# Top-k attention with two MLP blocks: staging of the early scores, the values' middle chunk, and the place of the end flag

## The chip, the cores and the metric

The kernel runs on one core of one Trainium2 chip. The metric is the device time of one execution in microseconds (us), the median of several runs. The engines are called as in the profile: PE (TensorE, matmul), DVE (VectorE), ACT (ScalarE), POOL (GpSimd), SP (SyncE, which issues all the DMAs of this kernel).

## What is computed

Four batches, eight heads, 576 positions, head size 64, all in fp32. Each score row keeps its 32 largest entries. The attention's output goes through a gated block (a causal convolution of five taps makes the gate) and then through a token and a channel MLP.

```python
scores = scale * np.matmul(q, k.transpose(0, 1, 3, 2))
kth = np.partition(scores, -top_k, axis=-1)[..., -top_k:-top_k + 1]
scores = np.where(scores >= kth, scores, -1e9)
attn = softmax(scores)
x = np.matmul(attn, v)                      # (B, S, 512) after the heads are joined
gate = 1 / (1 + np.exp(-causal_conv5(x, conv_w)))
x = (gate * (x @ w_val)) @ w_out
u = x + (np.maximum(x.transpose(0, 2, 1) @ w_tok1, 0) @ w_tok2).transpose(0, 2, 1)
out = u + np.maximum(u @ w_ch1, 0) @ w_ch2
```

## The kernel before

The program is written by a planner. Every operation is added to an `Order` with its engine, an assumed cost, the keys that it reads and writes, and a priority. `Order.issue` (L143) makes eight rounds of list scheduling, forwards and backwards, keeps the shortest plan, and emits the instructions in the plan's order. On the chip each engine then runs its own instructions strictly in that order: an instruction that has to wait holds back all that stand behind it on its engine.

Work is cut by batch b, by pair p of heads (four pairs to a batch) and by unit u (five to a pair). A unit u < 4 is two tiles of 128 query rows, one per head; the unit u = 4 is one tile that holds the last 64 rows of both heads. `all` (L782) adds, for each batch, the 20 units of attention (`attn`, L372), then the gated block (`gate`, L606), then the token and channel MLP (`mix`, L691). The attention of batch b + 1 is planned beside gate and mix of batch b. Nothing stands beside the attention of batch 0 but the decoding of weights; nothing but gate and mix is left at the end.

One unit goes like this. `scores` (L301) makes q·k in two halves of 288 columns: PE writes PSUM (`Sp`, or in batch 0 `Sp` and `mo[0]` in turn), ACT copies each half to SBUF (`S`, L332, or L349 for u = 4), and the second half's product must wait for the first half's copy, since it takes the same PSUM. Between the halves DVE folds the row (`fold`, L468) and then finds the 32 largest (`topk`, L481 to L500). ACT makes the mask (L414), POOL applies it (L416), ACT takes the exponential and its sum (L419), PE transposes it (L428), ACT copies that (L433), PE multiplies by the values (`pv`, L439 to L445), and ACT moves the result to `xf` (L449).

Three places matter here.

- **Early scores.** Batch 3's scores are made already in batch 0's attention, one unit of `pre` (L358) after each unit of `attn`, with `pq` (queries and keys), `mo[1]` (PSUM) and a single tile `pst` into which ACT copies both halves. One DMA (L370) writes `pst` to a DRAM tile `sd`, which batch 3 reads back in place of its own score products (L389). The next unit's first copy may write `pst` only when that DMA has landed. `gate` of batch 0 takes `mo[0]` and `mo[1]` after them. The tiles `fs` (`f0` to `f3`), the running x of gate and mix, hold nothing until the gate of batch 0.
- **The values.** `vt` holds ten chunks of 64 columns: chunk 0 to 4 for one head, 5 to 9 for the other (shifted by 64 rows). For u < 4 `pv` issues eight products of 128 rows by 64 columns (L441, L442; one fp32 product shows as two records) and two on 64 by 64 (L444, L445) for the middle chunk, where the two heads share a chunk of rows.
- **The flag.** `fold` and `topk` leave in `bad` whether any row of any unit broke the shortcut. After the whole plan, `run` (L765) reduces `bad` on DVE (L771), transposes on PE (L772), reduces again (L773), compares (L775). All five engines load the flag (`values_load`, L776) and branch over a second, slow version of the program (L777).

Of the kernel before, what the change touches and what calls it, by code (L numbers as in the profile page):

```python
# [10 lines left out]
I32 = mybir.dt.int32  # L11
# [156 lines left out]
class Builder:  # L168
    def __init__(self, ctx, tc, qk, v, w_val, conv, w_out, w_tok1, w_tok2, w_ch1, w_ch2, out):
# [10 lines left out]
        self.vt = [T(f"v{i}", [128, 10, 64]) for i in range(2)]  # L180
# [13 lines left out]
        self.cst = T("cst", [1, 1])  # L194
# [15 lines left out]
        self.pq, self.pst = T("pq", [128, 2, S]), T("pst", [128, 2, S])  # L210
# [11 lines left out]
        self.cnt = dict(mo=0, tf=0, ring=0, rT=0, st=0, wa=0, unit=0, tile=0, load=0)  # L222
# [82 lines left out]
    def scores(self, u, Sp, kSp, q, k, P, R, St, kS, then):  # L305

        nc = self.nc
        if u < 4:

            for n in range(2):  # L310
# [19 lines left out]
                if n:  # L330
                    then()
                self.act(S, lambda c0=c0: nc.scalar.activation(St[:, :, c0:c0 + 288], Sp[:, :, 0:288], AF.Copy),  # L332
# [15 lines left out]
        for n in range(2):  # L348
            self.act(288, lambda n=n: nc.scalar.activation(St[:, 0, 288 * n:288 * n + 288], Sp[:, n, 0:288], AF.Copy),  # L349
                     [kSp], kS[n] + [kSp] * n)  # L350
            if n == 0:
                then()
# [5 lines left out]
    def pre(self, c, u):  # L358

        nc = self.nc  # L360
        t = self.pq
        R = [("pq", x) for x in range(2)]
# [4 lines left out]
        st = self.pst  # L367
        k = [("pst", x) for x in range(2)]
        self.scores(u, self.mo[1], ("mo", 1), t[:, 0], t[:, 1], None, R, st, [k[n:n + 1] for n in range(2)], lambda: None)
        self.dma(2.3 * w, lambda: nc.sync.dma_start(self.sd[c, u], st[:, 0:w]), k, [("sd", c, u)])  # L370

    def attn(self, p, u):  # L372
# [13 lines left out]
        if b == PRE and self.fast:  # L386
            x = (p % 4, u)
            o = St[:, 0:w]
            self.dma(2.3 * w, lambda x=x, o=o: nc.sync.dma_start(o, self.sd[x]), [("sd", *x)],  # L389
# [49 lines left out]
        def pv():  # L439
            for y in range(4):  # L440
                nc.tensor.matmul(o[0:64, 0:n], vt[:, y], a[:, y * 128:y * 128 + n], start=(y == 0), stop=False)  # L441
                nc.tensor.matmul(o[64:128, 0:n], vt[:, 5 + y], e[:, y * 128 + g:y * 128 + 128], start=(y == 0), stop=False)  # L442
            r = slice(64, 128) if w == 2 else slice(0, 64)
            nc.tensor.matmul(o[0:64, 0:n], vt[0:64, 4], e[0:64, 512:512 + n], start=False, stop=True)  # L444
            nc.tensor.matmul(o[64:128, 0:n], vt[r, 4 if w == 2 else 9], e[r, 512 + g:640], start=False, stop=True)  # L445

        self.pe(1.39 if w == 2 else 0.877, pv, [x[1] for x in pts] + [("v", s)],
# [317 lines left out]
    def run(self):  # L765
        nc = self.nc
        with self.tc.manual_schedule():
            self.setup()
            self.all(True)
            m = self.nb[0][:, 0, 0:1]  # L770
            nc.vector.tensor_reduce(m, self.bad, mybir.AxisListType.XYZ, OP.max)  # L771
            nc.tensor.transpose(self.PT[0:1, 0:128], m, self.ident)  # L772
# [4 lines left out]
        with self.tc.If(again == 1):  # L777
            with self.tc.manual_schedule():
                self.o = Order()
                self.all(False)  # L780
# [70 lines left out]
```

## Time and profile before

| | us |
|---|---|
| median of 3 runs | 940.01 |
| the 3 runs | 930.69, 940.01, 940.73 |
| the profiled execution, its own time | 931.29 |
| its span, first to last instruction | 929.4 |
| PE busy | 844.8 (91%) |
| DVE busy | 767.3 (83%) |
| ACT busy | 574.1 (62%) |
| POOL busy | 410.8 (44%) |
| mean granted clock of PE, of full speed | 0.964 |

Busy time counts the instructions of an engine and not its waits. A stretch in which an engine is busy nearly all the time is bound by it; where no engine is, the order in which the engines wait for one another sets the pace. Line numbers are those of the kernel before.

### The profile page before, as it was taken

To read this page: it belongs to the slowest core of one execution; us is meant where nothing else is said; L and a number is where in the kernel's file an instruction comes from. 1 tells how busy PE (TensorE), PEld (TensorE's weight loads), DVE (VectorE), ACT (ScalarE), POOL (GpSimd) and SP (SyncE) were. 2 spreads that over 40 slices of the span, in tenths; PEclk is the share of its full clock that TensorE was granted. 3 is DMA by queue.
4 is the path that set the end of the run, shared out by engine and by line. 5 is a ranking of instruction groups with operands and counts; after the bars stand their busy time and mean duration, and the time that the engine had idled before them with its cause. 6 is when DMAs were issued, how large, how long until landed. Compare 5 with 4: busy or idle time off the path is not lost.

```text
span 929.4 us, 18849 instructions
## 1 busy us (share of the span) xinstructions
PE 844.8 (91%) x6713; PEld 718.7 (77%) x6713; DVE 767.3 (83%) x2653; ACT 574.1 (62%) x1271; POOL 410.8 (44%) x369
## 2 busy tenths in 40 slices
PE   5777777998999998989999999989999999889996
PEld 2444445797887987769788888979799998879996
DVE  8789979788999999997699998999899997712222
ACT  4878796856887775685677675474665665322100
POOL 1333354776976676474264332274353443402000
PEclk8999895999999998989999999999999999999998
DMA  5434321256335545614213324743345545222452
GB/s 190 168 119 153 127 70 52 96 204 226 117 106 196 187 184 189 228 53 130 78 31 124 106 84 148 239 145 129 105 156 200 189 132 165 91 91 91 160 162 98
DMA packets 39496, 128.22 MB, mean 138 GB/s; under 512 B 4512, under 2 KB 4768, under 8 KB 39392
## 3 DMA queue, kind: packets, MB, share of 16 engines
q1 hardware_dynamic: 39392, 126.92, 40.4%
q8 instruction: 55, 0.90, 0.4%
q14 instruction: 49, 0.40, 0.1%
HBM read 94.79 MB, written 32.11 MB: 137 GB/s over the span
## 4 chain that ended last, share of the span: by engine, by line
PE 61%; DVE 15%; ACT 12%; DMA 7%; POOL 2%; issue 2%; SPq 0%; ACTq 0%; DVEq 0%; POOLq 0%
PE mo L580 14%; PE mo L581 13%; PE mo L582 12%; PE PT L428 6%; PE PT L441 5%; DMA sd<-pst 5%; DVE f L667 4%; PE Sp L317 3%; PE mo L659 2%; ACT E L419 2%; ACT pst L332 2%; PE PT L444 2%; ACT W L414 2%; DMA stage<-in_w_ch_dram 2%; DVE top L498 2%
## 5 line engine op out<-in xcount | busy, mean ns | idle before, releaser
L580 PE MATMUL mo<-r,ring 128*128 128x288 f32 x1024 | 318.6, 311 | 4.6 <-DVE xf L647 2.6
L581 PE MATMUL mo<-r,ring 128*128 128x288 f32 x1024 | 305.6, 298 | 3.5 <-POOL r L518 2.0
L582 PE MATMUL mo<-r,ring 128*128 128x288 f32 x1024 | 304.4, 297 | 0.5 <-POOL ring L518 0.5
L416 POOL TENSOR_TENSOR E<-S,W 128x576 f32<-128x576 f32 x144 | 208.4, 1464 | 131.4 <-ACT W L414 129.1
L580 PEld LDWEIGHTS mo<-r,ring 128*128 128x128 f32 x1024 | 194.6, 190 | 17.0 <-issue 7.3
L581 PEld LDWEIGHTS mo<-r,ring 128*128 128x128 f32 x1024 | 194.9, 190 | 6.3 <-POOL r L518 3.5
L582 PEld LDWEIGHTS mo<-r,ring 128*128 128x128 f32 x1024 | 194.7, 190 | 1.1 <-POOL ring L518 1.1
L419 ACT ACTIVATE E<-E,nb 128x576 f32<-128x576 f32 x144 | 111.3, 774 | 23.5 <-POOL E L416 23.0
L498 DVE MAX8 top<-Z 128x8 f32<-128x168 f32 x432 | 125.6, 323 | 0.2
L433 ACT ACTIVATE pT<-PT 128x512 f32<-128x512 f32 (+1 forms) x144 | 94.2, 654 | 46.9 <-PE PT L428 46.2
L428 PE MATMUL PT<-ident,E 128*128 128x128 f32 x656 | 104.0, 288 | 15.8 <-ACT pT L433 7.8
L414 ACT ACTIVATE W<-S,nb 128x576 f32<-128x576 f32 x144 | 106.1, 770 | 1.5 <-POOL E L416 1.5
L428 PEld LDWEIGHTS PT<-ident,E 128*128 128x128 f32 x656 | 76.9, 145 | 37.1 <-ACT pT L433 15.2
L524 ACT ACTIVATE r<-mo 128x576 fp32r<-128x576 f32 (+2 forms) x76 | 46.9, 633 | 84.8 <-PE mo L582 81.3
L487 POOL TENSOR_TENSOR bad<-X,top 128x6 f32<-128x6 f32 (+1 forms) x80 | 26.3, 328 | 158.4 <-DVE top L498 150.2
L441 PE MATMUL PT<-pT,v 128*64 128x128 f32 (+1 forms) x640 | 83.3, 275 | 9.3 <-ACT pT L433 9.3
L500 DVE MATCH_REPLACE8 Z<-top,Z 128x168 f32<-128x168 f32 x288 | 89.9, 318 | 0.0
L441 PEld LDWEIGHTS PT<-pT,v 128*64 128x64 f32 x640 | 65.1, 140 | 26.4 <-ACT pT L433 15.1
L442 PE MATMUL PT<-pT,v 128*64 128x128 f32 (+1 forms) x640 | 83.3, 275 | 0.0
L689 DVE TENSOR_TENSOR f<-mo,f 128x576 f32<-128x576 f32 x64 | 47.9, 749 | 38.3 <-PE mo L582 38.2
L518 POOL TENSOR_TENSOR r<-f,r 128x576 fp32r<-128x576 f32 x32 | 50.5, 1587 | 60.5 <-ACT r L517 60.4
L533 DVE SCALAR_TENSOR_TENSOR r<-mo,r 128x576 fp32r<-128x576 f32 (+1 forms) x42 | 31.2, 743 | 44.0 <-ACT r L524 44.0
(133 smaller groups left out, 1710.1 us busy)
## 6 DMA issues: line engine op xcount, KB each, us to landing
ring<-ch1d SPq DMA_DIRECT2D x36, 512.0 KB, 3.5
ring<-ch2d SPq DMA_DIRECT2D x36, 512.0 KB, 3.5
stage<-in_w_ch_dram SPq DMA_DIRECT2D x24, 512.0 KB, 3.9
sd<-pst SPq DMA_DIRECT2D x16, 576.0 KB, 2.8
S<-sd SPq DMA_DIRECT2D x16, 576.0 KB, 4.8
qk<-in_qk_dram SPq DMA_DIRECT2D x24, 288.0 KB, 3.2
ch1d<-ring SPq DMA_DIRECT2D x12, 512.0 KB, 4.0
ch2d<-ring SPq DMA_DIRECT2D x12, 512.0 KB, 3.5
```

The source lines that it names most:

```text
L414: self.act(S, lambda W=W, x=x, t=t: nc.scalar.activation(W, x, AF.Relu, bias=nb[:, t, 1:2], scale=-BIG), kx + [(kN, 1)], [kW], True)
L416: self.pool(S, lambda W=W, x=x, E=E: nc.gpsimd.tensor_tensor(E, x, W, op=OP.subtract), kx + [kW], [kE])
L419: self.act(S + 110, lambda E=E, d=d, t=t: nc.scalar.activation(E, E, AF.Exp, bias=nb[:, t, 0:1], scale=0.125, accum_out=d), [kE, (kN, 0)], ...
L428: nc.tensor.transpose(self.PT[:, y * 128:(y + 1) * 128], E2[:, k * 128:(k + 1) * 128], self.ident)
L433: self.act(n, lambda pT=pT, n=n: nc.scalar.activation(pT[:, 0:n], self.PT[:, 0:n], AF.Copy), kp, [kP])
L441: nc.tensor.matmul(o[0:64, 0:n], vt[:, y], a[:, y * 128:y * 128 + n], start=(y == 0), stop=False)
L442: nc.tensor.matmul(o[64:128, 0:n], vt[:, 5 + y], e[:, y * 128 + g:y * 128 + 128], start=(y == 0), stop=False)
L498: self.dve(n, lambda src=src, o=o: v.max(o, src), k, [(kM, q)] + [kM] * (q in (0, 3)))
L500: self.repl(n, lambda src=src, o=o: v.match_replace(out=z, in_to_replace=o, in_values=src, imm_value=NEG), k + [(kM, q)], [kz])
L580: nc.tensor.matmul(o, wh, xh, start=(x == 0), stop=False)
L581: nc.tensor.matmul(o, wh, xl, start=False, stop=False)
L582: nc.tensor.matmul(o, wl, xh, start=False, stop=(x == last))
```

## The change

Batch 3's early scores no longer go through `pst`. Each unit takes two of the four `fs` tiles (one for u = 4), the next unit the other two. A 128 x 2 x 288 copy becomes two copies of 128 x 288, one per tile, and a unit's DMA becomes one DMA per tile. `pq` becomes two tiles that take turns by pair. `pst` goes.

The values get an eleventh chunk on the host: chunks 4 and 5 are now one block of 128 by 128 with head one's middle rows in its upper left, head two's in its lower right, and zeros elsewhere. For u < 4 one product with this block takes the place of the two on 64 by 64. For u = 4 nothing changes but the index.

The flag is computed by planned operations (`check`), which `all` adds after batch 3's attention and ahead of its gate; it goes to tiles of its own (`worst`, `cst`, `flag`) and uses the last 128 columns of `PT`. The load and the branch stay at the end.

```diff
-        self.vt = [T(f"v{i}", [128, 10, 64]) for i in range(2)]
+        self.vt = [T(f"v{i}", [128, 11, 64]) for i in range(2)]
...
-        self.cst = T("cst", [1, 1])
+        self.cst, self.flag, self.worst = T("cst", [1, 1]), T("flag", [1, 1], I32), T("worst", [128, 1])
...
-        self.pq, self.pst = T("pq", [128, 2, S]), T("pst", [128, 2, S])
+        self.pq = [T(f"pq{i}", [128, 2, S]) for i in range(2)]
...
                 if n:
                     then()
+                if isinstance(St, list):
+                    for t in range(2):
+                        self.act(288, lambda c0=c0, t=t: nc.scalar.activation(St[t][:, c0:c0 + 288], Sp[:, t, 0:288], AF.Copy),
+                                 [kSp], kS[n][t:t + 1] + [kSp] * t)
+                    continue
...
     def pre(self, c, u):
...
-        t = self.pq
-        R = [("pq", x) for x in range(2)]
+        t = self.pq[c % 2]
+        R = [("pq", c % 2, x) for x in range(2)]
...
-        st = self.pst
-        k = [("pst", x) for x in range(2)]
-        self.scores(u, self.mo[1], ("mo", 1), t[:, 0], t[:, 1], None, R, st, [k[n:n + 1] for n in range(2)], lambda: None)
-        self.dma(2.3 * w, lambda: nc.sync.dma_start(self.sd[c, u], st[:, 0:w]), k, [("sd", c, u)])
+
+        j = self.cnt["pre"] % 2 * 2
+        self.cnt["pre"] += 1
+        st, k = self.fs[j:j + w], [("f", j + x) for x in range(w)]
+        self.scores(u, self.mo[1], ("mo", 1), t[:, 0], t[:, 1], None, R, st, [[(x, n) for x in k] for n in range(2)],
+                    lambda: None)
+        for x in range(w):
+            self.dma(2.3, lambda x=x: nc.sync.dma_start(self.sd[c, u][:, x], st[x]), [(k[x], n) for n in range(2)] + [k[x]],
+                     [("sd", c, u, x)])
...
         def pv():
             for y in range(4):
                 nc.tensor.matmul(o[0:64, 0:n], vt[:, y], a[:, y * 128:y * 128 + n], start=(y == 0), stop=False)
-                nc.tensor.matmul(o[64:128, 0:n], vt[:, 5 + y], e[:, y * 128 + g:y * 128 + 128], start=(y == 0), stop=False)
-            r = slice(64, 128) if w == 2 else slice(0, 64)
+                nc.tensor.matmul(o[64:128, 0:n], vt[:, 6 + y], e[:, y * 128 + g:y * 128 + 128], start=(y == 0), stop=False)
+            if w == 2:
+
+                nc.tensor.matmul(o, vt[:, 4:6].rearrange("p a b -> p (a b)"), e[:, 512:640], start=False, stop=True)
+                return
             nc.tensor.matmul(o[0:64, 0:n], vt[0:64, 4], e[0:64, 512:512 + n], start=False, stop=True)
-            nc.tensor.matmul(o[64:128, 0:n], vt[r, 4 if w == 2 else 9], e[r, 512 + g:640], start=False, stop=True)
-
-        self.pe(1.39 if w == 2 else 0.877, pv, [x[1] for x in pts] + [("v", s)],
+            nc.tensor.matmul(o[64:128, 0:n], vt[0:64, 10], e[0:64, 512 + g:640], start=False, stop=True)
+
+        self.pe(1.33 if w == 2 else 0.877, pv, [x[1] for x in pts] + [("v", s)],
                 ["o"], 0.1, 0.88)
...
-            m = self.nb[0][:, 0, 0:1]
-            nc.vector.tensor_reduce(m, self.bad, mybir.AxisListType.XYZ, OP.max)
-            nc.tensor.transpose(self.PT[0:1, 0:128], m, self.ident)
-            nc.vector.tensor_reduce(self.cst, self.PT[0:1, 0:128], mybir.AxisListType.X, OP.max)
-            f = self.tf[0][0:1, 0:1].bitcast(I32)
-            nc.vector.tensor_scalar(f, self.cst, 0.0, None, op0=OP.is_gt)
-        again = nc.values_load(f, min_val=0, max_val=1, skip_runtime_bounds_check_because="is_gt gives 0 or 1")
+        again = nc.values_load(self.flag, min_val=0, max_val=1, skip_runtime_bounds_check_because="is_gt gives 0 or 1")
...
+    def check(self):
+
+        v = self.nc.vector
+        t = self.PT[0:1, 896:1024]
+        self.prio = self.at + 20
+        self.dve(480, lambda: v.tensor_reduce(self.worst, self.bad, mybir.AxisListType.XYZ, OP.max),
+                 [("bad", i) for i in range(NP * 5)], ["worst"])
+        self.pe(0.11, lambda: self.nc.tensor.transpose(t, self.worst, self.ident), ["worst"], ["o"])
+        self.dve(128, lambda: v.tensor_reduce(self.cst, t, mybir.AxisListType.X, OP.max), ["o"], ["cst"])
+        self.dve(1, lambda: v.tensor_scalar(self.flag, self.cst, 0.0, None, op0=OP.is_gt), ["cst"], ["flag"])
...
             self.dp, self.dd, self.da, self.dl = MOFF
+            if b == B - 1 and fast:
+                self.check()
             self.gate(b, self.at + OFF)
...
+    m = np.zeros((NP, 128, 2, D), v.dtype)
+    m[:, 0:64, 0], m[:, 64:128, 1] = v[:, 0:64, 4], v[:, 64:128, 4]
+    v = np.concatenate([v[:, :, 0:4], m, v[:, :, 5:10]], axis=2)
```

## Rows read from the trace of the kernel before

**Rows 1.** Windows: us, then busy us (instructions) of each engine, clock, DMA share, GB/s.

```profile
0.00:128.00 128.00, 90.19 (x669) 52.74 (x669) 107.69 (x466) 97.78 (x223) 44.54 (x54) 0.92 0.41 149
128.00:160.00 32.00, 23.68 (x162) 15.11 (x160) 31.90 (x133) 23.78 (x56) 14.09 (x14) 0.68 0.10 30
160.00:790.00 630.00, 606.21 (x5003) 532.71 (x4999) 582.47 (x2000) 427.09 (x953) 336.13 (x293) 0.99 0.44 146
790.00:921.00 131.00, 124.33 (x887) 118.03 (x886) 43.45 (x54) 25.45 (x40) 16.06 (x11) 0.99 0.37 120
...
25.00:50.00 25.00, 18.98 (x155) 11.69 (x154) 20.06 (x87) 21.78 (x51) 9.53 (x9) 0.97 0.38 142
...
75.00:100.00 25.00, 19.20 (x146) 11.16 (x146) 24.97 (x113) 19.90 (x49) 7.46 (x8) 0.93 0.41 150
```

**Rows 2.** The chain that ended last, by line, from the page.

```profile
PE mo L580 14%; PE mo L581 13%; PE mo L582 12%; PE PT L428 6%; PE PT L441 5%; DMA sd<-pst 5%; DVE f L667 4%; PE Sp L317 3%; PE mo L659 2%; ACT E L419 2%; ACT pst L332 2%; PE PT L444 2%; ACT W L414 2%; DMA stage<-in_w_ch_dram 2%; DVE top L498 2%
```

**Rows 3.** Waits of 0 to 165 us: waited for; total us, times, longest.

```profile
ACT pst L332 <- DMA sd<-pst: 17.4, 12, 2.7
...
DVE y L468 <- ACT E L419: 6.9, 1, 6.9
DVE y L468 <- ACT pst L332: 4.9, 1, 4.9
...
DVE den L624 <- ACT E L419: 3.7, 1, 3.7
```

**Rows 4.** Timeline, 50 to 62 us: start, duration, instruction, idle before and releaser.

```profile
54.81 0.65 ACT L332 ACTIVATE pst<-mo 128x576 f32<-128x576 f32 x1 [2.45 <-DMA sd<-pst]
...
59.26 0.17 DVE L624 TENSOR_SCALAR den<-den 128x9 f32<-128x9 f32 x1 [3.66 <-ACT E L419]
```

**Rows 5.** Early scores: DMAs by tile `pst` (issues; landing), and SP's waits.

```profile
L370 SPq DMA_DIRECT2D sd<-pst x20: 319/326/334, 11.7 to 125.4; - x20
...
DMA to landing us min/median/max: 2.1/2.8/4.6
...
SPq L370 <- ACT pst L332: 63.9, 13, 7.6
```

**Rows 6.** Chain in order of time, 0 to 300 us: start, us on chain, what.

```profile
34.04 0.59 PE PT L428 x4
...
62.94 0.60 ACT pst L349 x2
...
75.34 0.55 ACT pst L332
```

**Rows 7.** Timeline of PE where the gate of batch 0 begins.

```profile
162.48 0.44 PE L633 MATMUL mo<-ident,rhl 128*41 128x128 f32 x1
```

**Rows 8.** Timeline of PE, the end of one value product.

```profile
127.65 0.27 PE L441 MATMUL PT<-pT,v 128*64 128x128 f32 x1
...
127.76 0.27 PE L441 MATMUL PT<-pT,v 128*64 128x128 f32 x1
...
127.97 0.32 PE L444 MATMUL PT<-pT,v 64*64 64x128 f32 x1
...
128.34 0.76 PE L323 MATMUL Sp<-qk 64*128 64x288 f32 x4
```

**Rows 9.** The end: timeline, then lines 776 and 777 (durations in ns, starts).

```profile
921.15 0.76 DVE L689 TENSOR_TENSOR f<-mo,f 128x576 f32<-128x576 f32 x1 [2.42 <-PE mo L582]
...
923.14 0.14 DVE L775 TENSOR_SCALAR t<-cst 1x1 int32<-1x1 f32 x1
...
L776 PEldq TENSOR_LOAD <-t x1: 487/487/487, 923.4 to 923.4; - x1
...
L777 PEldq COMPARE_BRANCH  x1: 4347/4347/4347, 924.0 to 924.0; - x1
...
L777 DVEq EVENT_SEMAPHORE  x1: 21/21/21, 927.5 to 927.5; - x1
L777 PEldq EVENT_SEMAPHORE  x1: 51/51/51, 928.4 to 928.4; - x1
```

More of the change, by code (lines that the diff above doesn't have):

```diff
@@ L221, in __init__ @@
         self.mo = [self.ps.tile([128, 2, 512], F32, name=f"mo{i}") for i in range(2)]
-        self.cnt = dict(mo=0, tf=0, ring=0, rT=0, st=0, wa=0, unit=0, tile=0, load=0)
+        self.cnt = dict(mo=0, tf=0, ring=0, rT=0, st=0, wa=0, unit=0, tile=0, load=0, pre=0)
         self.slot = {}
@@ L348, in scores @@
         for n in range(2):
-            self.act(288, lambda n=n: nc.scalar.activation(St[:, 0, 288 * n:288 * n + 288], Sp[:, n, 0:288], AF.Copy),
+            z = St[0] if isinstance(St, list) else St[:, 0]
+            self.act(288, lambda n=n, z=z: nc.scalar.activation(z[:, 288 * n:288 * n + 288], Sp[:, n, 0:288], AF.Copy),
                      [kSp], kS[n] + [kSp] * n)
@@ L388, in attn @@
             o = St[:, 0:w]
-            self.dma(2.3 * w, lambda x=x, o=o: nc.sync.dma_start(o, self.sd[x]), [("sd", *x)],
+            self.dma(2.3 * w, lambda x=x, o=o: nc.sync.dma_start(o, self.sd[x]), [("sd", *x, y) for y in range(w)],
                      [(x, n) for x in kS for n in range(2)])
```

## The prediction

> **What bounds the kernel now.** I read the windows first, to see which engine is full where. In the long middle, from 160 to 790 us, PE works 606 of 630 us, and from 790 to 921 it works 124 of 131 [rows 1]. There, only less PE work or an earlier start moves the end. From 0 to 128 us it is another kernel: PE works 90 of 128, DVE 108, ACT 98, and none is full [rows 1]. Something makes them wait for one another. From 128 to 160 DVE works 31.9 of 32 [rows 1]: there DVE is the bound. The window from 0 to 128 is the one in which the early scores run (their DMAs start between 11.7 and 125.4 us [rows 5]).
>
> The page's chain says the same from the other end: PE's mixing products carry it, but 5% of 929.4 us, some 46 us, is a DMA, the one from `pst` to `sd`, and 2% more the copies ahead of it [rows 2]. A chain overstates what can be saved, since another path lies just beneath, so I went to the waits of the first 165 us. ACT stood still 17.4 us in 12 waits for this DMA [rows 3]. ACT runs in order, so what stands behind the waiting copy (score copies, masks, exponentials of the unit that DVE needs next) is late too. DVE shows it: 6.9 and 4.9 us before folds, 3.7 us before a row of denominators, all put down to ACT [rows 3], 15.5 us together, out of the 20.3 that DVE is idle up to 128 us [rows 1]. One case can be followed: ACT waits 2.45 us for the DMA until 54.81, and DVE then sits 3.66 us until 59.26, behind an exponential that ACT reached late [rows 4].
>
> The gate of batch 0 starts on PE at 162.48 [rows 7], just behind the stretch in which DVE is full. From there PE is the bound to the end. So what DVE wins before 160 us, PE's whole remaining line should win.
>
> **Part one, the early scores.** The wait is removed by giving a unit's tiles back one unit later. 20 units in about 114 us [rows 5] are 5.7 us apart, and a DMA lands 2.8 us after its issue (4.6 at most) [rows 5]. With one buffer, the copy of the next unit must come after that; with two, it has some 11 us. So I set the wait for the DMA at nothing. What becomes late next is the pair PE and ACT on `mo[1]`, still one tile: the second half's product waits for the first half's copy as before.
>
> It adds ACT work. A 576-column copy holds ACT 0.55 us and two of 288 columns 0.60 [rows 6], so 16 units with two copies each cost 32 x 0.05 = 1.6 us. ACT has 97.8 + 23.8 = 121.6 us of work in 160 us [rows 1], 123.2 after. How far can it be pressed? In 75 to 100 us ACT was busy 19.9 of 25, 80%, with DVE full; in 25 to 50 us 21.8 of 25, 87%, with DVE losing time [rows 1]. At 80% the 160 us shrink to 154, a gain of 6; at 87% to 141.6, a gain of 18, of which DVE's waits allow only 15.5. The price lies between 6 and 15.5; I take the middle, 10.5, since the trace has both loads.
>
> The 16 DMAs more (36 for 20) cost SP 0.33 us of issue each [rows 5], 5.3 us on an engine that sat 63.9 us waiting for these very copies [rows 5]: hidden by that wait. The second `pq` tile takes a reload off the same line; it is in the 10.5. The `f` tiles are first written by the gate behind 162 us [rows 7], and the last early DMA went out at 125.4 [rows 5]; even 20 us later it would cost nothing. After the early scores end, PE's granted clock drops (0.68 from 128 to 160, between the levels of 1.2 and 2.4 GHz), yet DVE is full there [rows 1], so I price a longer stretch of that at nothing.
>
> **Part two, the value product.** The last paired product begins at 127.76, 0.11 after the one before it; the 64 by 64 pair begins 0.21 later, at 127.97, and the next work at 128.34 [rows 8]. The middle chunk thus takes 0.37 us, and the step into it 0.1 more than a step within the eight. The new product's nearest row is the transposes, 128 by 128 with 128 columns: four take 0.59 us on the chain, 0.15 each [rows 6], so its two records take 0.30. That saves 0.07. If the step of 0.1 goes too, 0.17; if it comes twice, a loss of 0.03. I take 0.05, nearer the lower end, because the layout still changes. Only the 48 such units of batches 1 to 3 run where PE is the bound: 48 x 0.05 = 2.4 us, bounds -1.4 and 8.2.
>
> The row shows a step of 0.21 where the layout changes against 0.11 where it doesn't [rows 8]. The Trainium skill (TensorEngine Tiling (Array Packing), Key Properties) says that a change of tiling mode drains the engine. By that rule the step stays, since the block is again another mode than 128 by 64, and the part is worth 48 x 0.07 = 3.4; the row alone would leave 8.2 open. The values' DMA grows by a tenth and is loaded a pair ahead; nothing.
>
> **Part three, the flag.** Now: the last add starts at 921.15 and takes 0.76, the flag is there at 923.28, PE loads it (0.49), reaches the branch at 924.0, and that takes 4.35, to 928.35; PE's last event follows at 928.4, the span ends at 929.4 [rows 9]. After: the flag is long there. PE, whose last product is over at 921.15, would be at its branch at 921.8 and through at 926.1. DVE cannot load before 921.91; its end event came 3.5 us after its branch (927.5 against 924.0) [rows 9], so it comes at about 926.1 too. PE's event then at 926.2 to 926.6: a gain of 1.8 to 2.2. I take 1.8; nothing if the plan leaves the check at the end. The moved chain, 1.4 us from 921.91 to 923.28 [rows 9], falls between 790 and 921, where DVE has 87 us free [rows 1]; on the path it would cost those 1.4.
>
> The row shows 4.35 us in the branch alone. The Trainium skill (Runtime: NRT & Kernel Launch, Instruction fetch mechanics) says that a taken branch out of the prefetched window waits for a fetch of its target. By that rule the 4.35 stays wherever the flag is made, and only the 1.8 goes; read as a wait for the flag's own chain, the row would let some 4 go.
>
> **Sum.** 10.5 + 2.4 + 1.8 = 14.7 us. The profiled execution took 931.29 us, 1.9 of it outside the span; 931.3 - 14.7 = 916.6. That execution agrees with the lowest of the three runs (930.69); the other two (940.01, 940.73) lie 9 us higher, for no reason that the trace shows. If the median after falls like that one, it is 925. I forecast 920, nearer the lower, since the sum is made there.
>
> **Rivals.**
>
> *Given back.* ACT, not DVE, is the true limit of the first 160 us. For it: ACT was at 87% in one window [rows 1], and gets more instructions. Against it: at 80% DVE was full. Then the first part gives 3 to 6, the product about nothing, the flag 1.8: 931.3 - 5 to 8 = 923 to 926, or 932 to 935 on the upper runs. That the change doesn't do what it says (two units in flight still wait, since ACT takes them in pairs) belongs here, with the same time.
>
> *All of it.* DVE's 15.5 come back whole, the product gives 8.2, the flag 2.3: 931.3 - 26 = 905. For it: the DVE waits all name ACT. Against it: every price at its best end.
>
> *Slower, by SP's queue.* SP too runs in order. It waited up to 7.6 us for one early copy [rows 5]; now each unit has two such waiting DMAs, and the loads of the next pair's queries and keys stand behind them. Four pairs are loaded in this stretch. If each came 7.6 us late for PE, that is 30 us: 931.3 - 14.7 + 30 = 947. It turns the sign when each is more than 14.7 / 4 = 3.7 us late beyond its slack, and makes it slower by 1% from 6.0 on. Against it: pairs are loaded one ahead, and DVE's waits name ACT, no load [rows 3].
>
> **How the numbers follow.** The forecast has 0.53, with a range of its own from 908 to 929 (the upper end on the upper runs). Given back has 0.30, all of it 0.07, slower 0.10. The range runs from 904, all of it, to 936, given back on the upper runs; it leaves out the slower case and the outer edges of the others. A measurement of this kernel tells about 1%, 9 us, from no change. Faster by more is the forecast and all of it, 0.60; within 1% is given back, 0.30; slower 0.10.
>
> **What would show it.** ACT's waits for the DMA into `sd` gone from the first 165 us; DVE's three waits for ACT shorter than 6 us in sum; the first gate product on PE near 152 us in place of 162.5; if PE starts there and the end does not move, the gain was lost in the middle, where PE is then idle more than 24 of 630 us. One product in place of L444 and L445, with less than 0.37 us to the next work. PE's branch some 0.7 us behind its last product, now 2.9, with the compare far ahead. If ACT's waits are gone and the gate starts at 160 all the same, part one's reasoning is wrong; if `qk` loads show up as what PE waits for in the first 150 us, SP's queue was it.

## The result and the profile after

| | before | after |
|---|---|---|
| median, us | 938.86 of 4 runs (930.69 to 940.73) | 900.48 of 4 runs (898.78 to 902.92) |
| span of the profiled execution, us | 929.4 | 897.8 |
| PE busy, us | 844.8 | 830.4 |
| mean granted clock of PE | 0.964 | 0.985 |
| first product of batch 0's gate, us | 162.5 | 143.3 |
| last transfer to the output issued, us | 922.0 | 892.4 |

The changed kernel is faster by 3.9%: the ratio is 0.9609, 95% interval 0.9547 to 0.9671. That is the direction that the prediction gave, and more than twice its size: 31.6 us between the two spans, 38 between the medians, where the sum had 14.7. The time lies below the range.

The two milestones of the table cut the span into three parts. The start of batch 0's gate comes 19.2 us earlier ([rows 7], and the line below). From there to the last output takes 749.1 us in place of 759.5, 10.4 less. What follows the last output takes 5.4 in place of 7.4, 2.0 less.

```profile
143.26 0.27 PE L647 MATMUL mo<-ident,rhl 128*41 128x128 f32 x1
```

First, the early part. Windows of the kernel after; the columns are those of [rows 1].

```profile
0.00:25.00 25.00, 16.89 (x66) 8.88 (x67) 21.85 (x94) 14.92 (x37) 5.12 (x12) 0.93 0.63 221
25.00:50.00 25.00, 20.84 (x171) 12.70 (x169) 24.65 (x111) 24.11 (x63) 11.18 (x12) 1.00 0.42 148
50.00:75.00 25.00, 20.21 (x172) 12.66 (x172) 24.83 (x109) 23.54 (x64) 10.20 (x12) 1.00 0.47 150
75.00:100.00 25.00, 19.82 (x166) 12.14 (x166) 24.90 (x109) 23.14 (x60) 10.05 (x11) 1.00 0.35 122
100.00:125.00 25.00, 19.51 (x166) 12.19 (x163) 25.00 (x104) 24.52 (x66) 14.01 (x13) 1.00 0.39 132
125.00:143.30 18.30, 13.05 (x99) 9.20 (x99) 18.23 (x81) 15.25 (x36) 10.02 (x11) 0.81 0.26 80
```

Read the third busy column, DVE. From 25 us on it is full in every window. Two of the same windows of the kernel before, which the prediction did not show, have 21.3 and 16.8 of 25:

```profile
50.00:75.00 25.00, 18.42 (x149) 11.38 (x147) 21.30 (x95) 19.78 (x49) 8.60 (x11) 0.93 0.37 128
...
100.00:125.00 25.00, 18.05 (x143) 10.49 (x144) 16.84 (x70) 21.19 (x48) 11.75 (x11) 0.93 0.37 133
```

The waits of DVE in the first 165 us of the kernel after (waited for; total us, times, longest), with PE's longest wait for a load there, and the early scores' transfers:

```profile
DVE xf L661 <- PE mo L656: 1.1, 1, 1.1
...
DVE y L482 <- PE Sp L323: 1.0, 1, 1.0
...
DVE den L638 <- ACT E L430: 0.5, 1, 0.5
...
PE Sp L323 <- DMA qk<-in_qk_dram: 4.5, 1, 4.5
```

```profile
L380 SPq DMA_DIRECT2D sd<-f x36: 319/324/390, 12.4 to 126.0; - x36
```

The three waits of [rows 3], 15.5 us, have shrunk to 0.5, and ACT's 17.4 us of waiting for the transfer to `sd` are gone: no such line is left. PE's wait of 4.5 us for queries and keys is that of the very first load and stands in the kernel before as well (4.6); the only other wait of PE for a load in this stretch is 0.3 us, for `pq`. The 36 transfers, 16 more than in [rows 5], were issued in the same stretch, and no wait names one of them.

The stretch behind the gate, windows of before and then of after:

```profile
0.00:162.50 162.50, 116.36 (x839) 69.55 (x839) 141.43 (x603) 123.22 (x281) 60.29 (x68) 0.87 0.35 125
162.50:922.00 759.50, 728.15 (x5876) 649.05 (x5874) 624.93 (x2048) 450.88 (x990) 350.52 (x301) 0.99 0.42 141
```

```profile
0.00:143.30 143.30, 110.32 (x829) 67.77 (x829) 139.46 (x603) 125.49 (x318) 60.59 (x70) 0.96 0.43 145
143.30:892.40 749.10, 720.11 (x5759) 649.43 (x5757) 624.59 (x2051) 451.66 (x986) 342.76 (x300) 0.99 0.43 144
```

PE works 8.0 us less behind the gate (728.15 to 720.11) and is idle 2.4 less (31.35 to 28.99): the 10.4. About 3 of the 8.0 are the new product, as the next views show. About 1 is the clock: PE was busy at 1.2 GHz for 15.5 us behind the gate before, for 13.4 after. The other 4 have moved: PE's work ahead of the gate, with what ran at 1.2 GHz counted at half its time, grew from 99.0 to 105.3 us, although that stretch is shorter by 19. (The 4 and the 6.3 need not agree to the microsecond, since PE's records overlap and their ends are modelled.)

The value product. The timeline of PE in the kernel after, at the end of three of them:

```profile
126.45 0.27 PE L452 MATMUL PT<-pT,v 128*64 128x128 f32 x1
...
126.56 0.27 PE L452 MATMUL PT<-pT,v 128*64 128x128 f32 x1
...
126.77 0.49 PE L456 MATMUL PT<-pT,v 128*128 128x128 f32 x2
```

```profile
300.48 0.49 PE L456 MATMUL PT<-pT,v 128*128 128x128 f32 x2
300.81 0.38 PE L439 MATMUL PT<-ident,E 128*128 128x128 f32 x2
...
311.20 0.49 PE L456 MATMUL PT<-pT,v 128*128 128x128 f32 x2
311.62 0.40 PE L317 MATMUL Sp<-qkh 64*128 64x288 f32 x2
```

One line stands in place of L444 and L445. The step into it is 0.21 (126.56 to 126.77), the step within the pairs 0.11, as in [rows 8]. From there to the next work it takes 0.33 before a transpose and 0.42 before score products, which have 64 rows and so another form; it was 0.37. A whole value product, from its first record to the next work, took 1.39 us before. At full clock it now takes 1.27 before a mixing product (25 of these), 1.35 before a transpose (12) and 1.44 before a score product (14).

The end. The last add, and then the load of the flag (L784) and the branch over the slow version (L785), durations in ns and starts:

```profile
773.03 0.13 DVE L799 TENSOR_SCALAR flag<-cst 1x1 int32<-1x1 f32 x1
```

```profile
891.55 0.76 DVE L703 TENSOR_TENSOR f<-mo,f 128x576 f32<-128x576 f32 x1 [2.42 <-PE mo L596]
```

```profile
L784 PEldq TENSOR_LOAD <-flag x1: 488/488/488, 889.0 to 889.0; - x1
...
L785 SPq EVENT_SEMAPHORE  x8: 17/17/17, 895.9 to 896.4; - x8
...
L785 PEldq COMPARE_BRANCH  x1: 3862/3862/3862, 889.6 to 889.6; - x1
...
L785 DVEq COMPARE_BRANCH  x1: 72/72/72, 892.2 to 892.2; - x1
L785 SPq COMPARE_BRANCH  x1: 45/45/45, 893.4 to 893.4; - x1
L785 PEldq EVENT_SEMAPHORE  x1: 51/51/51, 893.5 to 893.5; - x1
L785 DVEq EVENT_SEMAPHORE  x1: 21/21/21, 895.5 to 895.5; - x1
```

The flag is there at 773. PE reaches its branch at 889.6, while its last products still run, and the branch takes 3.86 us all the same. Against [rows 9] the roles have changed: PE's event, last before (928.4), is now the first of these, and SP's and DVE's come last.

### The profile page after: what moved, and what is told of

Same layout as the page of the kernel before. It is cut to its first block, busy times and chain, and to the rows that moved or that the text cites. A ratio compares the mean times of both kernels' runs of the same rounds, so it can differ in the third digit from the quotient of the medians.

```text
span 897.8 us, 18631 instructions
## 1 busy us (share of the span) xinstructions
PE 830.4 (92%) x6585; PEld 717.2 (80%) x6585; DVE 764.0 (85%) x2653; ACT 577.2 (64%) x1303; POOL 403.3 (45%) x369
## 4 chain that ended last, share of the span: by engine, by line
PE 45%; DVE 10%; ACT 4%; POOL 3%; issue 2%; DMA 0%; POOLq 0%; DVEq 0%; ACTq 0%
PE mo L594 11%; PE mo L595 11%; PE mo L596 11%; PE PT L439 4%; PE PT L452 3%; DVE f L681 2%; PE Sp L317 2%; POOL r L532 1%; PE PT L456 1%; DVE top L512 1%; POOL E L427 1%; DVE Z L514 1%; DVE y L482 1%; ACT r L538 1%; DVE f L703 1%
## 5 line engine op out<-in xcount | busy, mean ns | idle before, releaser
L427 POOL TENSOR_TENSOR E<-S,W 128x576 f32<-128x576 f32 x144 | 208.3, 1462 | 103.1 <-ACT W L425 94.3
L444 ACT ACTIVATE pT<-PT 128x512 f32<-128x512 f32 (+1 forms) x144 | 94.4, 656 | 42.1 <-PE PT L439 41.2
L439 PE MATMUL PT<-ident,E 128*128 128x128 f32 x656 | 99.8, 280 | 11.5 <-ACT pT L444 4.9
L501 POOL TENSOR_TENSOR bad<-X,top 128x6 f32<-128x6 f32 (+1 forms) x80 | 21.1, 265 | 156.5 <-DVE top L512 132.5
L452 PE MATMUL PT<-pT,v 128*64 128x128 f32 (+1 forms) x640 | 81.9, 272 | 8.4 <-ACT pT L444 7.8
L452 PEld LDWEIGHTS PT<-pT,v 128*64 128x64 f32 x640 | 64.0, 138 | 25.6 <-ACT pT L444 17.7
L453 PE MATMUL PT<-pT,v 128*64 128x128 f32 (+1 forms) x640 | 81.9, 272 | 0.0
```

The source lines that it names most:

```text
L427: self.pool(S, lambda W=W, x=x, E=E: nc.gpsimd.tensor_tensor(E, x, W, op=OP.subtract), kx + [kW], [kE])
L439: nc.tensor.transpose(self.PT[:, y * 128:(y + 1) * 128], E2[:, k * 128:(k + 1) * 128], self.ident)
L444: self.act(n, lambda pT=pT, n=n: nc.scalar.activation(pT[:, 0:n], self.PT[:, 0:n], AF.Copy), kp, [kP])
L453: nc.tensor.matmul(o[64:128, 0:n], vt[:, 6 + y], e[:, y * 128 + g:y * 128 + 128], start=(y == 0), stop=False)
```

## The experiments

Two theories stood after the result. By the first the early scores' wait was the whole matter, and the prediction had only priced it too low: ACT can be pressed further than the middle of its two loads, and DVE's idle time comes back nearly whole. By the rival the surplus came from elsewhere, from the new order that the planner made, from the product, or from PE's clock. All ratios are against the kernel before on the same chip.

### Each part alone

The kernel before with part one alone (the `fs` tiles and the two `pq`):

```diff
+        st, k = self.fs[j:j + w], [("f", j + x) for x in range(w)]
...
+        t = self.pq[c % 2]
```

> The kernel before with the change's first part alone (early scores through the four x tiles, two units in flight, two pq tiles). Theory A (the first 160 us): DVE's idle time there comes back, the first gate product on PE starts near 143 us in place of 162.5, and the end moves by at least those 19 us; what else the full change gained (some 11 us between the first and the last gate) is the order that the planner finds once DVE runs ahead, so this kernel keeps most of it: 28 to 35 us faster in all. Theory B (the value product): the 11 us in the middle belong to the block product, so this kernel gains 19 to 21 us and no more.

Measured: 904.63 us (903.35 to 908.47), ratio 0.9677 [0.9622, 0.9732]. Windows up to the gate and behind it:

```profile
0.00:142.70 142.70, 109.52 (x859) 65.80 (x859) 138.38 (x600) 124.40 (x317) 60.53 (x69) 0.97 0.40 141
142.70:894.40 751.70, 726.72 (x5856) 648.63 (x5854) 618.09 (x2052) 451.33 (x987) 346.77 (x300) 0.99 0.42 143
```

Part one alone gives 31.6 us of the 36 to 38. The gate starts at 142.7, DVE is idle 4.3 us before it (142.70 less 138.38). Behind the gate PE is idle 25.0.

The kernel before with the block product alone (its planned cost 1.33, as in the change):

```diff
+                nc.tensor.matmul(o, vt[:, 4:6].rearrange("p a b -> p (a b)"), e[:, 512:640], start=False, stop=True)
```

> The kernel before with the block product alone, its planned cost 1.33 in place of 1.39 as in the change. Theory A: the product is worth nothing by itself, since in the trace of after the next work starts 0.33 to 0.42 us after it, where the pair took 0.36 to 0.37; within 5 us of before, and what is left is the new order of the plan. Theory B: 48 products save 0.24 us each, some 11 us faster. My prediction's term: 2.4 us.

Measured: 922.40 us (920.79 to 924.22), ratio 0.9851 [0.9797, 0.9904]. That is 13.8 us for a part that can save 3 by its own rows. Theory B came near in size, but its step of 0.24 us for each product stands in no row.

The kernel before with the flag's part alone:

```diff
+            if b == B - 1 and fast:
+                self.check()
```

> The kernel before with the flag made behind the last attention, and nothing else. Both theories: the time from the last add to the end of the span shrinks from 8.3 to about 6.2 us, so 2 us faster, if the plan's order elsewhere stays. A larger move would be the plan's order.

Measured: 936.10 us of 10 runs, ratio 0.9999 [0.9970, 1.0028]. The end did shorten, from 7.4 us behind the last output to 5.5. But for the four operations of the flag the order is that of the kernel before, on every engine. So the order took nothing back; the 2 us are less than the interval can tell (2.6 us either way). In one and the same order the gate began at 165.7 in this trace and at 162.5 and 160.6 in two of the kernel before.

The kernel after without part one (product and flag only):

```diff
-        st, k = self.fs[j:j + w], [("f", j + x) for x in range(w)]
+        st = self.pst
```

> The kernel before with the block product and the early flag, but the early scores as before: the changed kernel less its first part. Theory A: the first gate near 162 us, the time 918 to 926, so that the first part is worth 18 to 26 us beside the other two. If the parts do not add up (alone they gave 31.6, 13.8 and 0.1 us, 45 together, against 36 to 38 for the whole), it is outside that.

Measured: 926.13 us (920.96 to 930.44), ratio 0.9896 [0.9828, 0.9965]; the gate at 165.8. So part one is worth 25.6 us where the other two are there already (926.1 to 900.5), 31.6 where they aren't. Up to the flag this kernel has the order of the product alone (922.40), and with the flag it is 3.7 slower, its runs 9.5 us apart: the flag's 2 us show in the traces' ends only. The parts alone sum to 31.6 + 13.8 + 0.1 = 45.5, the whole is 36 to 38: they overlap.

### Is it the second unit in flight?

The kernel after, with every unit in the same pair of `fs` tiles:

```diff
-        j = self.cnt["pre"] % 2 * 2
+        j = 0
```

> The changed kernel, but every early unit takes the first two x tiles, so that one unit is in flight and the next copy waits for its DMAs again; two pq tiles, split copies, block product and early flag stay. Theory A (the wait for the DMA is what held ACT, and DVE behind it): the waits of ACT for the DMA come back (some 17 us), the first gate product goes back from 143 to near 160 us, and the time to 920 to 930. Theory C (the second pq tile, or the plan's order, made the gain): the first gate stays near 145 and the time below 908.

Measured: 925.82 us (924.01 to 929.18), ratio 0.9897 [0.9850, 0.9943]. Its waits in the first 165 us, and its window up to the gate:

```profile
ACT f L334 <- DMA sd<-f: 14.8, 10, 4.0
...
DVE y L482 <- ACT nb L413: 5.3, 1, 5.3
...
DVE y L482 <- ACT pT L444: 4.3, 1, 4.3
```

```profile
0.00:161.60 161.60, 116.24 (x811) 70.39 (x811) 139.97 (x604) 126.15 (x317) 61.40 (x70) 0.89 0.37 129
```

ACT's wait for the transfer is back, the long waits of DVE for ACT with it, and the gate at 161.6. That is the time of the kernel without part one (926.13): with one unit in flight the smaller transfers, the copies cut in two and the second `pq` bring nothing. Of the 26.8 us between the two spans (924.6 and 897.8) 18.3 are the later gate. Behind it PE is busy 5.3 us more, mostly because 6.9 us more of its work ran at 1.2 GHz, and idle 3.2 more. The order of the plan changed with the edit, so these 8.5 us aren't shown to come from the wait.

The kernel after with one `pq` (queries and keys of the early scores not loaded ahead):

```diff
-        t = self.pq[c % 2]
+        t = self.pq[0]
```

> The changed kernel with a single pq tile, so that the next pair's queries and keys of the early scores are loaded only when the last early product of this pair is over. Theory A: three reloads of some 4 us, in which DVE has other work; within 4 us of the changed kernel's 900. Theory C: half of the gain or more is lost, above 915.

Measured: 913.70 us (910.62 to 916.26), ratio 0.9759 [0.9712, 0.9806], 13 more than the kernel after, where a few were expected. The early part is as expected, the gate at 143.9. The loss is behind it:

```profile
143.90:386.10 242.20, 229.89 (x1765) 198.64 (x1763) 223.14 (x740) 172.27 (x385) 162.06 (x138) 0.95 0.48 167
```

The kernel after has 235.3 us for this stretch (143.3 to 378.6, batch 0's last output), with a clock of 0.99. Here it takes 242.2 with PE at 0.95: 20.8 us of PE's work ran at 1.2 GHz in place of 6.8, and PE was idle 12.3 in place of 9.3. From the gate to the end 37.3 us of PE's work ran at 1.2 GHz, in the kernel after 13.4: that is 11.9 of the 15.0 us between the spans (912.8 and 897.8), and the mean clock of the four runs is 0.969 to 0.972, of the kernel after 0.977 to 0.985. So what is lost here is mostly PE's clock behind the gate. The last load into `pq` starts at 94.3 us; the order of the plan is another. That the order is what held the clock down isn't shown, nor that the second `pq` is worth 13 us.

The kernel after with the four `fs` tiles joined to two, so that a unit has one copy per half and one transfer, as before, but two units are in flight:

```diff
-        self.fs = [T(f"f{i}", [128, S]) for i in range(4)]
+        self.f2 = [T(f"f{i}", [128, 2, S]) for i in range(2)]
+        self.fs = [self.f2[i // 2][:, i % 2] for i in range(4)]
...
+        self.dma(2.3 * w, lambda: nc.sync.dma_start(self.sd[c, u], st[:, 0:w]), [(x, n) for x in k for n in range(2)] + k,
```

> The changed kernel with the four x tiles made as two tiles of two, so that an early unit needs one copy of 2 x 288 columns per half and one DMA, as in the kernel before, with two units still in flight. Theory A: 1.6 us less of ACT's work and 16 DMAs fewer in the first 143 us, where ACT is 88% busy: the first gate at 141 to 144, the time within 4 us of the changed kernel. If splitting the copies was what kept ACT's line short, slower by over 5 us.

Measured: 909.34 us (907.34 to 913.82), ratio 0.9710 [0.9667, 0.9753], 9 slower than the kernel after although ACT has fewer instructions. The gate began at 147.5, with DVE idle for 7.3 us up to there (3.8 in the kernel after). And 7.6 us followed the last output in place of 5.4, though the flag was made at 770.6: SP's last events, which stand at 895.9 to 896.4 in the kernel after, run from 908.2 to 910.6. These are 6 of the 14 us between the profiled spans (912.0 and 897.8); 4.8 more are in the last stage (144.0 us from batch 2's last output to batch 3's, 139.2 after), at a clock of 0.95 against 0.99. The order of the plan is another here too. So whether the joined copies made the gate late, or whether they would pay in the same order, stays open.

### Order alone

The kernel before with the planned cost of the value product changed, and no instruction; and the kernel after with that cost put back:

```diff
-        self.pe(1.39 if w == 2 else 0.877, pv, [x[1] for x in pts] + [("v", s)],
+        self.pe(1.33 if w == 2 else 0.877, pv, [x[1] for x in pts] + [("v", s)],
```

> The kernel before with one number of the planner changed: the assumed cost of a value product 1.33 in place of 1.39. Not one instruction differs, only their order. Theory A: the order alone moves the time by some us either way (up to 6), and by it the effect of the product can be told from e2. Theory B: no difference above 2 us, so that the order explains nothing of the middle.

> The changed kernel with one number of the planner put back: the assumed cost of a value product 1.39 in place of 1.33. Not one instruction differs, only the order. If the changed kernel's 900 is what the removed wait is worth, the time stays within 4 us. If part of it is the plan's luck, it is up to 15 us slower, as the kernels with one pq tile (913.7) and with paired copies (909.3) were, with the first gate still near 143 us.

Measured: 935.25 us of 10 runs, ratio 0.9997 [0.9966, 1.0028] for the first; 898.54 us (893.94 to 901.84), ratio 0.9618 [0.9569, 0.9667] for the second. The order that this cost brings is worth nothing that shows here, although it starts the gate later (167.8 in the first one's trace, 162.5 and 160.6 in two of the kernel before): starts of the gate are to be compared within one order. The first has exactly the order of the product alone, apart from the product itself, so the 13 us between those two (935.25 and 922.40) come with the product, not with the planner's order.

### Why runs of the kernel before differ

The kernel before once more, not changed, with a profile.

> The kernel before once more, for a second trace of it: its runs spread from 930.6 to 941.4 us, those of the changed kernel from 898.8 to 902.9. If the spread is PE's clock, the stretches at the lower clock lie elsewhere or are longer in a slower execution, with the order and the waits for the DMA unchanged; if it is the DMAs, the landings of the early scores' DMAs differ.

Measured: 938.6 us, span 936.8, against 929.4 in the trace that the prediction read. The waits for the transfer are nearly the same (16.6 us, 17.4 there). The gate begins 1.9 us earlier, at 160.6; the next stretch takes 7.0 us more, the rest 2.3 more. Its window here, the same stretch in the first trace, and the first four convolution products of the gate, here and there:

```profile
160.60:401.20 240.60, 228.31 (x1773) 196.00 (x1771) 220.35 (x721) 167.39 (x371) 161.47 (x134) 0.96 0.48 169
```

```profile
162.50:396.10 233.60, 222.33 (x1773) 191.84 (x1771) 216.95 (x714) 167.36 (x371) 161.16 (x134) 0.98 0.50 173
```

```profile
165.92 2.29 PE L659 MATMUL mo<-xf,diag 128*128 128x288 f32 x4 [0.92 <-DVE xf L647]
```

```profile
166.18 1.24 PE L659 MATMUL mo<-xf,diag 128*128 128x288 f32 x4 [0.92 <-DVE xf L647]
```

The same instructions take 2.29 and 1.24 us, nearly the ratio of the two levels, 1.2 and 2.4 GHz; both windows hold 1773 of them, and PE's busy time differs by 6.0 of the 7.0 us. What PE did before: it was busy 27.85 of the 37.5 us from 125 to 162.5, at a granted clock of 0.69 (in the first trace). There the clock comes back with the gate, at 163.3 us; here at 171.7.

Could this be the surplus too? PE's clock up to the gate is 0.87 before and 0.96 after. So the kernel before was given products that nobody reads, behind its transposes (3 each) and value products (4 each) of batch 0, into columns of `PT` that are not used:

```diff
+    def keep(self, b, n):
+        for _ in range(n if b == 0 and self.fast else 0):
+            self.nc.tensor.transpose(self.PT[:, 768:896], self.ident, self.ident)
```

> The kernel before, order unchanged, with PE kept busier up to the first gate: behind each tile's transposes in batch 0 three more, and behind each value product four more, of the identity into PSUM that nobody reads (some 190 of 0.15 us). If PE's lower clock is part of what the kernel before pays (before and just behind the first gate, and the spread of its runs), the granted clock of the first 162 us rises from 0.87 to above 0.95, the runs come closer together, and the time falls to 925 to 931 although the waits for the DMA stay. If the clock costs nothing there, the time stays at 936 or rises by the added work.

Measured: 938.34 us of 10 runs, ratio 1.0028 [1.0004, 1.0052].

```profile
0.00:164.30 164.30, 128.13 (x1005) 82.34 (x1005) 140.26 (x597) 123.88 (x281) 59.56 (x68) 0.95 0.34 122
```

The clock rose to 0.95, the gate didn't come earlier, and the runs spread as before. So nothing of the surplus came back with the clock. But the added products are work too, and this alone doesn't show that the lower clock is free. The same products in the kernel after:

> The changed kernel with the same added transposes. Its granted clock up to the first gate was 0.96 already, so little is left to gain: 896 to 903. If PE's queue matters more than its clock, the added work holds back the score products and the first gate comes later than 145 us, the time above 905.

Measured: 909.95 us (907.71 to 911.81), ratio 0.9721 [0.9671, 0.9770]: 9.5 us slower than after, the gate at 154.8 in place of 143.3. DVE is idle 11.7 us up to there in place of 3.8. With 19 us more of work on PE (128.86 busy, 110.32 without it) DVE comes late in the kernel after; in the kernel before 12 us more of busy time, part of it won back by the clock, left the gate where it was.

### Where the product's 13 us come from

The rivals here: PE's clock behind the gate, or the wait for the transfer. Both kernels of one order (product alone, planned cost alone) were run twice more, not changed (their edits stand above), for the traces.

> The block product alone, a second trace. It and the kernel with the order alone have the same instructions in the same order but for the middle product, and differ by 13 us (922.4 and 935.3). Measured directly, a value product and the step behind it take 1.27, 1.35 or 1.44 us by what follows, where the pair took 1.39: some 3 us in all. If the clock makes the other 10, the stretches at the lower clock behind the first gate stay short here (10 us of PE's busy time) and long with the pair (15 to 26), in each trace. If that was chance, they overlap.

> The order alone (pairs of products), a second trace, to be held against the second one of the block product: 931 to 937 us; PE busy at the lower clock for 15 us or more behind the first gate if the clock makes the difference, under 10 if not.

> The block product alone, a third trace: 920 to 925 us, at the lower clock for about 10 us of PE's busy time behind the first gate if the clock makes the difference.

> The order alone, a third trace: 931 to 937 us, at the lower clock for 15 us or more of PE's busy time behind the first gate if the clock makes the difference.

Measured: 922.80 and 922.58 us with the product, 934.86 and 934.19 without. PE's time at 1.2 GHz behind the gate was 9.9, 16.5 and 19.9 us in the three traces with it and 25.7, 22.8 and 6.7 without; the last one without has the least of all but is no faster, so the clock falls as the cause. What does part the two sets is the time up to the gate:

| | with the product, 3 traces | without, 3 traces |
|---|---|---|
| first product of the gate, us | 163.6, 161.6, 161.2 | 167.8, 170.1, 170.6 |
| DVE idle up to there | 19.1, 16.2, 16.0 | 22.2, 25.8, 27.2 |
| ACT waits for the transfer to `sd` (its L332 copies) | 13.6, 15.3, 15.2 | 17.6, 18.5, 19.9 |

Waits of the third trace with the product, then of the third without:

```profile
ACT pst L332 <- DMA sd<-pst: 15.2, 11, 2.7
...
DVE y L471 <- ACT nb L402: 5.2, 1, 5.2
...
DVE y L471 <- ACT E L419: 4.1, 1, 4.1
```

```profile
ACT pst L332 <- DMA sd<-pst: 19.9, 12, 2.7
...
DVE y L468 <- ACT nb L402: 9.0, 2, 8.1
DVE y L468 <- ACT E L419: 8.3, 1, 8.3
```

The gate comes 7.4 us earlier on the mean (162.1 against 169.5), of 11.5 between the spans. Of the 4 behind it 3 are the product's own. ACT's waits for the transfer differ by 4.0 on the mean (14.7 against 18.7), DVE's idle time by 8.0. A fourth trace in this order, that of product and flag, has the gate at 165.8, 22.6 us of DVE's idle time and 14.3 of ACT's waits: gate and waits still part the two sets, DVE's idle time no longer does.

The traces also show how a saving of under 0.1 us in each product can do this. The sets part first at one copy into `pst`, here in the third trace with the product, then without:

```profile
53.75 0.65 ACT L332 ACTIVATE pst<-mo 128x576 f32<-128x576 f32 x1 [0.57 <-DMA sd<-pst]
```

```profile
56.49 0.65 ACT L332 ACTIVATE pst<-mo 128x576 f32<-128x576 f32 x1 [2.72 <-DMA sd<-pst]
```

It waits for the eighth of the 20 transfers. The queues from this transfer's issue to its landing, in the same two traces (packets, MB, share; then the transfer, with its us to landing last):

```profile
q1 hardware_dynamic: 144, 0.59, 51.6%
issues: line engine op xcount, KB each, median us to landing
sd<-pst SPq DMA_DIRECT2D x1, 576.0 KB, 2.8
```

```profile
q8 instruction: 1, 0.02, 1.6%
...
sd<-pst SPq DMA_DIRECT2D x1, 576.0 KB, 4.9
```

Without the product, a block of the program (16 KB, `q8 instruction`) is loaded within the transfer, which lands 2.1 us later: the load runs to 54.1 us, and the transfer's last eight packets follow one another from there to 55.9. In the six traces of the kernel before, the planned cost alone and the flag alone, such a load falls into the eighth transfer and into the 15th, which land 4.4 to 5.2 and 3.7 to 4.5 us after their issue. In the four with the product it falls into neither: 2.8 and 2.1. The number of `q8` loads goes with the length of PE's program (55 before, 54 with the product, 56 with the transposes that nobody reads). So what the product gains up to the gate starts with the moments at which PE's program is loaded: luck, which another kernel need not have. With the extra transposes too those two transfers were in time (2.8 and 2.3); the loads fell into the 13th and the 16th (4.0 and 4.1), among others.

So the product's surplus goes through the same waits as part one's gain, and part one, which takes the waits away, leaves the product only its own. Part one alone (904.63) and the kernel after with its planned cost put back (898.54) have one order but for the flag's operations, and differ by 6.1 us for product and flag together, of which 2 are the flag's.

## Why the prediction was right or wrong

**What bounds.** Right. The first 160 us were a stretch in which engines waited for one another, PE carries the rest; 19.2 of the 31.6 us are in the earlier start of the gate, 10.4 behind it.

**Part one, the mechanism.** Right, in each of its steps: no wait for the transfer is left, DVE's three waits fell from 15.5 to 0.5 us, and with one tile pair in place of two the time is that without part one (925.8 and 926.1). SP's 16 transfers more cost nothing that shows.

**Part one, the size.** Wrong: 10.5 forecast, 25.6 to 31.6 measured. Three steps failed. (The middle of 6 and 15.5, by the way, is 10.75.) The first: "How far can it be pressed?" was asked of ACT, and answered between two loads, 80% and 87%, that the trace happened to have. ACT ran at 88% up to the gate (125.49 of 143.30) and at 98% from 100 to 125 us. The 87% came with DVE losing time and was read as a strain on ACT; it was the loss that part one removes. The engine to ask was DVE: up to 162.5 us it had 141.4 us of work, so the gate could start at about 141 and what idle time at the start was unavoidable; it starts at 143.3. The second: "of which DVE's waits allow only 15.5". DVE was idle 21.1 us before the gate and is idle 3.8 now, 3.2 of it in the first 25 us. The gain was 17.2 of idle time and 2.0 that the same 603 instructions of DVE took less (141.43 to 139.46). The short waits, which the prediction left out, went with the three long ones. The third: "what DVE wins before 160 us, PE's whole remaining line should win" was a lower bound. PE did 4 to 6 us more of its work before the gate than in the longer stretch of before, and was idle 2.4 less behind it. How much of what was gained behind the gate another order would keep isn't shown: other kernels without the wait took 898.5 to 913.7.

**Part two.** Its own saving was right: 2.4 forecast, about 3 by the three forms of the timeline (25 x 0.12 + 12 x 0.04 - 14 x 0.05 = 2.8 over the 51 seen at full clock). The step of 0.21 stayed, and before the score products a second step shows, 0.42 to the next work. That agrees with the Trainium skill (TensorEngine Tiling (Array Packing), Key Properties), which says that a change of tiling mode drains TensorE; that the step is this drain no trace shows. What failed is "only the 48 such units of batches 1 to 3 run where PE is the bound". In batch 0 of the kernel before, PE's program with the product was loaded at moments that held back two transfers less, and the gate came some 7 us earlier; alone the product gave 13.8. Together with part one it came out near the forecast: 6.1 us with the flag, in one order.

**Part three.** The size was right, 2.0 against 1.8. The path was not: PE was to be at its branch 0.7 us behind its last product, and the branch was to be last. It is there 1.9 us before that product ends (889.6 against 891.52); the last events are SP's and DVE's. Each comes about 3 us behind its own branch, and by that the end now goes. The branch on PE still took 3.86 us with the flag long there, so it is not a wait for the flag. That agrees with the Trainium skill (Runtime: NRT & Kernel Launch, Instruction fetch mechanics), by which a taken branch to a target outside the prefetched window waits until that is fetched; that the branch waits for this fetch isn't shown here.

**The number.** "For no reason that the trace shows" put 920 above the sum's 916.6. A second trace shows one reason: PE's clock in batch 0's gate, about 6 of the 7.4 us between two executions. The runs of the kernel after spread 4 us, not 10; that its higher clock (0.96 up to the gate, 0.87 before) makes the difference isn't shown, since at 0.95 the kernel before spread 9. So the correction went the wrong way; but the larger fault was the sum.

**The rivals.** "All of it" (905) was nearest and still too high; it took DVE's 15.5 for the whole. "Given back" fell with ACT at 98% and DVE full. "Slower, by SP's queue" fell: behind its first load PE waits 0.3 us for loads.

## What to carry to other kernels

Where no engine is full and a wait is to go, size the gain by the engine that will be full afterwards: its own busy time in the stretch, plus the start that can't be avoided, is the time to expect; the load that other engines show beside the wait tells nothing of how far they can go. An in-order engine's 17 us of waits for transfers went with 25 to 32 us of the kernel's time, the change of order included. With the waits in place, even the moment at which a block of the program was loaded counted, and a small saving on PE came with more than its own size; so parts of a change that meet in such a wait must not be summed. With a planned order, compare a part with a kernel of the same order before the part is given the credit or the blame, and read the order off the traces before it is blamed.

## What the runs showed of the hardware

- Two executions of one program differed by 7 us in 930 in one stretch, where the convolution's products ran at 1.2 GHz in one (2.29 us for four) and at 2.4 in the other (1.24). Raised from 0.87 to 0.95 up to the gate with extra products, where PE isn't the bound, the clock left the time at 1.0028 of before; what it would bring without that work isn't shown.
- A block product of 128 by 128 behind products of 128 by 64 pays a step of 0.21 us in place of 0.11, and 0.42 in place of 0.33 to the next work where that has 64 rows. In the three forms the whole value product takes 1.27 to 1.44 us against 1.39.
- A branch on PE over the program's slow version took 3.39 to 4.47 us in the 18 traces, with the flag ready 100 us ahead or just made; the other engines' branches are recorded at 0.05 to 0.07.
- A 16 KB load of the program (`q8 instruction`) within a transfer of 576 KB made it land 4.4 to 5.2 us after its issue in place of 2.8, within one of 288 KB 3.7 to 4.5 in place of 2.1 (six traces against four).
- ACT can be busy 98% of 25 us (24.52) with DVE full beside it, when no copy of it waits for a transfer.
